# Three due times of an attention and expert schedule: 17 to 17.2, 33.7 to 33.2 and 65.7 to 65.2 heads

## The chip, the core and the metric

One core of one Trainium2 chip runs the kernel. TensorE (PE in the profile) multiplies; its weight loads have a row of their own (PEld). VectorE (DVE), ScalarE (ACT) and GpSimd (POOL) do the elementwise work, and SyncE (SP) issues nearly all of the DMAs. The metric is the device time of one execution in microseconds (us), the median of several runs. A profile is taken of one further execution; its span runs from the first to the last instruction.

## The reference

```python
scores = scale * np.matmul(q, k.transpose(0, 1, 3, 2))    # q, k, v: 8 batches, 8 heads, 576 x 64
mask = block_i >= block_j                                 # blocks of 64 positions
scores = np.where(mask, scores, -1000000000.0)
scores = scores - np.max(scores, axis=-1, keepdims=True)
attn = np.exp(scores)
attn = attn / (np.sum(attn, axis=-1, keepdims=True) + 1e-09)
x = np.matmul(attn, v)                                    # then laid out as 4608 tokens x 512
h = x @ w_in                                              # 512 x 2048
g = h * (1.0 / (1.0 + np.exp(-1.702 * h)))
out = g @ w_out                                           # 2048 x 512
```

Block-causal attention on 64 heads feeds a two-layer feed-forward part, all in float32. A token's row of `x` needs all 8 heads of its batch.

## The kernel before

**Attention.** The 64 heads are taken two at a time, in 32 turns (`step(n)`). A turn scores five query chunks of pair n, named 0 to 4: chunk i has up to 128 queries and 64·(2i+1) keys. `score` multiplies into PSUM banks; `weigh` adds the mask and finds the row's extreme on DVE (L351) and takes the exponential on ACT (L358); `normalise` makes the reciprocal of the sum on DVE (L368, L371) and scales on POOL (L376) or, in late turns, for chunk 4 on DVE (L378). In late turns `turn` transposes the weights on DVE (L385, L390), and sixteen DMAs behind chunk 4 finish the transposition. `av(n-1)` (item V) multiplies the previous pair's weights with its values, and ACT copies the result into a ring of tokens `xr` (L450, L451). `prep(n+1)` (item L) transposes the next pair's q and k on DVE (L297) into one buffer `qk`.

**Order within a turn.** A string says at which slot each item stands. Pairs 0 to 3 and 4 to 7 have their own (with PE transposes a, B, C instead of DVE's), pair 8 has `HANDOVER`, and pairs 9 to 31, the late turns, have

```python
    "3+0/2+1 - - - V - - 4 - - - L -",
```

that is 13 slots: chunks 3, 0, 2, 1 at slot 0, V at slot 4, chunk 4 at slot 7, L at slot 11.

**Experts.** The tokens are cut into 12 tiles of 384, each tile into 16 chunks (`fc`) of 128 columns of `w_in`. To keep float32's accuracy each operand is split into a high and a low part, so a product takes three matmuls. A chunk of experts is 12 matmuls into one bank `hp` (tag "h", a single buffer), then ACT's tanh (L562), DVE's product `g` (L563), ACT's `gh` (L571), POOL's `gl` (L82), and later 9 matmuls into three banks `acc` (`second`, which runs behind the next chunk's `hp`). The next chunk's first `hp` matmul writes the bank that L563 reads, so it waits for L563. When a tile changes, `split` casts new tokens to `xh` on ACT (L498) and takes the remainder `xl` on DVE (L82); `xh` and `xl` are single buffers too. A tile may be split only when all heads of its batches are done (`heads_for`).

**What mixes the two.** `moe()` is a generator that emits chunks. Behind every slot of a turn `advance` draws from it until the planned time `state["t"]` has reached a limit `quota(pos)`; `pos` counts heads (2 to a turn). In late turns it stops only at a gate, which stands behind the 12 `hp` matmuls of a chunk, so attention items enter PE's order only there. `quota` interpolates between pairs of heads and tiles:

```python
TILES_BY = ((8.4, 0), (17, 1), (33.7, 4), (65.7, -2))
        return -1.0 if pos < xs[0] else np.interp(pos, xs, [ends[y if y >= 0 else y - 1] for y in ys])
```

A tile's planned time is 16 equal chunks; -2 stands for the end of the tenth tile. The 11th and 12th tiles need all 64 heads and come last, with no attention beside them. PE's matmuls keep the order in which they are emitted (`keep_in_program_order`). On DVE, ACT and POOL the framework orders the instructions by priority (L562, L563, L571 and `split` have a higher one), and each engine then runs its own in that order.

Of the kernel before, what the change touches and what calls it, by code (L numbers as in the profile page):

```python
# [33 lines left out]


WEIGHTS_BY = ((0, 0), (8, 13), (14.5, 32))
TILES_BY = ((8.4, 0), (17, 1), (33.7, 4), (65.7, -2))


@with_exitstack  # L40
def attention_moe_kernel(
# [540 lines left out]
    def quota(pos):  # L582
        xs, ys = zip(*TILES_BY)
        return -1.0 if pos < xs[0] else np.interp(pos, xs, [ends[y if y >= 0 else y - 1] for y in ys])
# [80 lines left out]
```

## Time and profile before

| | |
|---|---|
| time, median of 3 runs | 1123.53 us (1121.69 to 1123.55) |
| the profiled execution's own time | 1120.49 us |
| its span | 1118.6 us |
| PE, PEld busy | 1076.4 us (96%), 908.7 us (81%) |
| DVE, ACT, POOL busy | 583.0 us (52%), 498.6 us (45%), 406.7 us (36%) |
| mean granted TensorE clock | 0.992 |

Matmuls overlap in the records, so the time that a group of matmuls takes on PE is best read from the start of its first to the start of the next group. A row of a timeline gives the start, the time of the group, the engine and line, the operation, the tile written and those read, their shapes, and in brackets the idle time just before, with what ended it. A row of windows gives for each stretch its length, then each engine's busy time with the number of instructions, the granted TensorE clock, the DMA engines' mean share and GB/s.

### The profile page before, as it was taken

To read this page: it belongs to the slowest core of one execution; us is meant where nothing else is said; L and a number is where in the kernel's file an instruction comes from. 1 tells how busy PE (TensorE), PEld (TensorE's weight loads), DVE (VectorE), ACT (ScalarE), POOL (GpSimd) and SP (SyncE) were. 2 spreads that over 40 slices of the span, in tenths; PEclk is the share of its full clock that TensorE was granted. 3 is DMA by queue.
4 is the path that set the end of the run, shared out by engine and by line. 5 is a ranking of instruction groups with operands and counts; after the bars stand their busy time and mean duration, and the time that the engine had idled before them with its cause. 6 is when DMAs were issued, how large, how long until landed. Compare 5 with 4: busy or idle time off the path is not lost. (4 is left out here: it accounts for less than half of the span.)

```text
span 1118.6 us, 19977 instructions
## 1 busy us (share of the span) xinstructions
PE 1076.4 (96%) x6960; PEld 908.7 (81%) x6960; DVE 583.0 (52%) x1856; ACT 498.6 (45%) x1321; POOL 406.7 (36%) x509
## 2 busy tenths in 40 slices
PE   5969998999999999999999999999999999999998
PEld 3757776788888888888888888888888888899997
DVE  6776885545545555654555655645545654211210
ACT  5866776434534433534443543444434444322322
POOL 4665664333333332333333333333333233122222
PEclk9979999999999999999999999999999999999999
DMA  8734532332444432343443333344342332200000
GB/s 171 205 89 153 150 73 62 84 79 57 105 86 86 103 80 64 64 98 78 98 101 74 75 93 65 70 108 85 81 107 63 71 85 58 54 29 1 29 1 29
DMA packets 219365, 91.25 MB, mean 82 GB/s; under 512 B 197760, under 2 KB 197760, under 8 KB 219264
## 3 DMA queue, kind: packets, MB, share of 16 engines
q1 hardware_dynamic: 214528, 89.38, 34.0%
q10 hardware_dynamic: 4736, 0.59, 0.3%
q8 instruction: 55, 0.90, 0.3%
q14 instruction: 46, 0.38, 0.1%
HBM read 45.09 MB, written 9.44 MB: 49 GB/s over the span
## 5 line engine op out<-in xcount | busy, mean ns | idle before, releaser
L82 POOL TENSOR_TENSOR gl<-g,gh 128x384 fp32r<-128x384 f32 x192 | 194.7, 1014 | 551.5 <-ACT gh L571 449.1
L99 PE MATMUL hp<-xh,wih 128*128 128x384 f32 x768 | 264.7, 345 | 7.9 <-DVE g L563 6.9
L563 DVE SCALAR_TENSOR_TENSOR g<-g,hp 128x384 f32<-128x384 f32 x192 | 105.9, 552 | 319.1 <-ACT g L562 317.8
L99 PE MATMUL hp<-xh,wil 128*128 128x384 f32 x768 | 258.4, 336 | 0.1
L562 ACT ACTIVATE g<-hp 128x384 f32<-128x384 f32 x192 | 94.1, 490 | 359.8 <-PE hp L99 354.8
L99 PE MATMUL hp<-xl,wih 128*128 128x384 f32 x768 | 253.9, 338 | 0.4 <-DVE xl L82 0.4
L99 PE MATMUL acc<-woh,gh 128*128 128x512 f32 x576 | 233.9, 406 | 0.0
L99 PE MATMUL acc<-wol,gh 128*128 128x512 f32 x576 | 226.9, 394 | 0.0
L99 PEld LDWEIGHTS hp<-xh,wih 128*128 128x128 f32 x768 | 144.2, 188 | 34.1 <-DVE g L563 23.1
L99 PE MATMUL acc<-woh,gl 128*128 128x512 f32 x576 | 167.9, 393 | 0.3 <-POOL gl L82 0.3
L571 ACT CAST gh<-g 128x384 fp32r<-128x384 f32 x192 | 98.4, 513 | 156.5 <-DVE g L563 156.4
L99 PEld LDWEIGHTS hp<-xh,wil 128*128 128x128 f32 x768 | 144.3, 188 | 6.5 <-POOL wil L82 0.7
L358 ACT ACTIVATE e<-e,mx 64x64 f32<-64x64 f32 (+4 forms) x240 | 132.3, 552 | 37.6 <-DVE mx L351 37.6
L376 POOL TENSOR_TENSOR e<-e,sm 64x64 f32<-64x64 f32 (+1 forms) x192 | 113.6, 612 | 95.0 <-DVE sm L371 46.5
L99 PEld LDWEIGHTS hp<-xl,wih 128*128 128x128 f32 x768 | 143.6, 188 | 1.3 <-DVE xl L82 1.3
L99 PE MATMUL bank<-qk 64*128 64x320 f32 (+4 forms) x768 | 122.5, 428 | 14.5 <-DVE qk L297 11.1
L99 PEld LDWEIGHTS acc<-woh,gh 128*128 128x128 f32 x576 | 107.9, 187 | 34.2 <-issue 10.5
L99 PEld LDWEIGHTS acc<-woh,gl 128*128 128x128 f32 x576 | 107.8, 188 | 25.9 <-POOL gl L82 1.2
L99 PEld LDWEIGHTS acc<-wol,gh 128*128 128x128 f32 x576 | 108.3, 188 | 16.7 <-POOL wol L82 0.3
L351 DVE CUSTOM_DVE_ANT_0 e<-bank,mask 64x64 f32<-64x64 f32 (+4 forms) x240 | 89.7, 417 | 56.9 <-PE bank L99 52.8
L385 DVE STREAM_TRANSPOSE turned<-e 128x384 f32<-128x384 f32 (+1 forms) x192 | 92.3, 499 | 48.8 <-POOL e L376 48.3
L99 PEld LDWEIGHTS bank<-qk 64*128 64x128 f32 x768 | 69.6, 193 | 54.2 <-issue 25.4
(50 smaller groups left out, 956.0 us busy)
## 6 DMA issues: line engine op xcount, KB each, us to landing
turned<-turned SPq DMA_DIRECT2D x192, 80.0 KB, 2.1
turned<-turned SPq DMA_DIRECT2D x96, 112.0 KB, 2.2
raw<-in_q_dram SPq DMA_DIRECT2D x128, 72.0 KB, 2.4
out_dram<-osb SPq DMA_DIRECT2D x36, 256.0 KB, 2.2
raw<-in_k_dram SPq DMA_DIRECT2D x120, 72.0 KB, 2.6
turned<-turned SPq DMA_DIRECT2D x96, 88.0 KB, 2.1
words<-in_moe_w_in_dram SPq DMA_DIRECT2D x16, 512.0 KB, 6.3
vp<-in_v_dram SPq DMA_DIRECT2D x60, 128.0 KB, 2.4
```

What stands on the lines that cost most here:

```text
L82: eng.tensor_tensor(out=out, in0=in0, in1=in1, op=ALU.subtract)
L99: return tc.keep_in_program_order(nc.tensor.matmul(**kw))
L351: nc.vector.tensor_tensor_reduce(out=e[0:m, hd, lo:hi], in0=s, in1=mk, op0=ALU.add, op1=ALU.min, scale=-0.125, scalar=3e38 if lo == 0 else ...
L358: nc.scalar.activation(out=e[0:m, hd], in_=e[0:m, hd], func=AF.Exp, scale=-1.0, bias=mx[0:m, i, hd : hd + 1], accum_out=sm[0:m, i, hd : hd ...
L376: nc.gpsimd.tensor_tensor(out=x, in0=x, in1=sc.to_broadcast([m, width(i)]), op=ALU.mult)
L385: nc.vector.transpose(out=tw[:, :, SLOT[i] : SLOT[i] + i, hd].rearrange("p b j c -> p j b c"), in_=e[:, hd, 0 : i * P],)
L562: nc.scalar.activation(out=g, in_=hp[:, 0:tt], func=AF.Tanh, scale=1.702)
L563: nc.vector.scalar_tensor_tensor(out=g, in0=g, scalar=1.0, in1=hp[:, 0:tt], op0=ALU.add, op1=ALU.mult)
L571: nc.scalar.copy(out=gh, in_=g)
```

## The change

```diff
-TILES_BY = ((8.4, 0), (17, 1), (33.7, 4), (65.7, -2))
+TILES_BY = ((8.4, 0), (17.2, 1), (33.2, 4), (65.2, -2))
```

Tile 0 is spread over 8.8 heads instead of 8.6. Tiles 1 to 3 get 16 heads instead of 16.7, which is 48/16 = 3 chunks a head or six a turn, where it was 48/16.7 = 2.87 or 5.75 a turn. Tiles 4 to 9 keep 32 heads, six chunks a turn, but start half a head earlier. The work itself is the same: as many matmuls, elementwise instructions and DMAs of the same shapes.

In the late turns DVE's order shows it. These are the rows around the start of chunk 4 in the turn of pair 22 (`turned<-e` is the end of chunks 2 and 1, `e,mx<-bank,mask 128x256` the first scores of chunk 4, `g<-g,hp` a chunk of experts). Before:

```order
L385 STREAM_TRANSPOSE turned<-e 128x2x4x32 x2
L390 STREAM_TRANSPOSE turned<-e 64x2x2x32
L563 SCALAR_TENSOR_TENSOR g<-g,hp 128x384
L351 ISA e,mx<-bank,mask 128x256
L351 ISA mx 128x1
L563 SCALAR_TENSOR_TENSOR g<-g,hp 128x384
```

With the change:

```order
L385 STREAM_TRANSPOSE turned<-e 128x2x4x32 x2
L390 STREAM_TRANSPOSE turned<-e 64x2x2x32
L351 ISA e,mx<-bank,mask 128x256
L351 ISA mx 128x1
L563 SCALAR_TENSOR_TENSOR g<-g,hp 128x384
```

One chunk's L563 no longer stands between the end of chunks 2 and 1 and chunk 4: chunk 4 comes one chunk of experts earlier.

Behind chunk 4 in the same turn, before:

```order
L297 STREAM_TRANSPOSE qk<-raw 128x576 x2
L368 TENSOR_SCALAR sm<-sm 128x2
L371 RECIPROCAL sm<-sm 128x2
L378 TENSOR_SCALAR e<-e,sm 128x576 x2
L385 STREAM_TRANSPOSE turned<-e 128x4x4x32 x2
L390 STREAM_TRANSPOSE turned<-e 64x2x2x32
L563 SCALAR_TENSOR_TENSOR g<-g,hp 128x384 x2
```

With the change:

```order
L297 STREAM_TRANSPOSE qk<-raw 128x576
L368 TENSOR_SCALAR sm<-sm 128x2
L371 RECIPROCAL sm<-sm 128x2
L378 TENSOR_SCALAR e<-e,sm 128x576 x2
L385 STREAM_TRANSPOSE turned<-e 128x4x4x32 x2
L390 STREAM_TRANSPOSE turned<-e 64x2x2x32
L563 SCALAR_TENSOR_TENSOR g<-g,hp 128x384
L297 STREAM_TRANSPOSE qk<-raw 128x576
L563 SCALAR_TENSOR_TENSOR g<-g,hp 128x384 x2
```

The second half of L moved behind the first L563, and three L563 instead of two follow before the next turn's scores.

The third place is the start of tile 7, in the turn of pair 24, again on DVE. With the change the rows of chunk 3's end and of the new tile are

```order
L563 SCALAR_TENSOR_TENSOR g<-g,hp 128x384
L82 TENSOR_TENSOR xl<-xr,xh 128x384 x3
L385 STREAM_TRANSPOSE turned<-e 128x3x4x32
L563 SCALAR_TENSOR_TENSOR g<-g,hp 128x384
L385 STREAM_TRANSPOSE turned<-e 128x3x4x32
L351 ISA e,mx<-bank,mask 128x192
```

and, some rows further,

```order
L385 STREAM_TRANSPOSE turned<-e 128x2x4x32
L82 TENSOR_TENSOR xl<-xr,xh 128x384
L385 STREAM_TRANSPOSE turned<-e 128x2x4x32
```

where before all four `xl` stood together behind chunks 2 and 1 (`L82 TENSOR_TENSOR xl<-xr,xh 128x384 x4`). The tile now starts on either side of V: three quarters of its tokens' columns are split ahead of V's result and the last quarter behind it. Also, one of chunk 3's two transposes stands ahead of the second L563 here; before, both stood behind it.

## The prediction

> **What bounds the kernel now.** First the profile's page, its span, its busy times and the slices.
>
> ```profile
> span 1118.6 us, 19977 instructions
> PE 1076.4 (96%) x6960; PEld 908.7 (81%) x6960; DVE 583.0 (52%) x1856; ACT 498.6 (45%) x1321; POOL 406.7 (36%) x509
> PE   5969998999999999999999999999999999999998
> ```
>
> PE is busy nearly throughout, and the work on it is the same after the change. So the time can move only by what PE stands still or waits inside its queue. The second view is the waits, cut to PE. From 218 to 445 us (pairs 9 to 15) it has this one row:
>
> ```profile
> PE hp L99 <- DVE g L563: 5.1, 6, 0.9
> ```
>
> Six waits of 0.85 us each; from 445 to 930 us (pairs 16 to 31) the same view has none. The third view is windows, cut at the first score matmul of a turn: two turns, three turns and fourteen turns, each turn of six chunks of experts.
>
> ```profile
> core 0: us, PE busy (x) PEld busy (x) DVE busy (x) ACT busy (x) POOL busy (x), PEclk, DMA share, GB/s
> 252.37:318.17 65.80, 64.09 (x421) 54.74 (x420) 35.76 (x118) 28.00 (x75) 21.64 (x28) 1.00 0.37 84
> 346.20:444.83 98.63, 96.09 (x631) 82.05 (x630) 52.88 (x175) 40.26 (x109) 32.42 (x42) 1.00 0.38 86
> 472.78:923.98 451.20, 450.89 (x2942) 381.94 (x2941) 247.47 (x818) 189.45 (x511) 151.36 (x196) 1.00 0.38 85
> ```
>
> A turn is 65.80/2 = 32.90 us and 98.63/3 = 32.88 us in the first two, and 451.20/14 = 32.23 us in the last, for the same matmuls at a granted clock of 1.00. So a turn with the wait costs 0.66 us more than one without (the rest of the 0.85 us comes back as small queueing that the others have). The question is which kind of turn the change makes.
>
> **What makes the wait.** A turn that has it, from chunk 4's matmuls on (PE, then ACT, then DVE):
>
> ```profile
> 429.81 1.24 PE L99 MATMUL bank<-qk 64*128 64x256 f32 x8
> 438.36 0.44 PE L99 MATMUL hp<-xh,wih 128*128 128x384 f32 x1 [0.85 <-DVE g L563]
> 435.52 0.49 ACT L562 ACTIVATE g<-hp 128x384 f32<-128x384 f32 x1 [0.73 <-PE hp L99]
> 430.90 0.31 DVE L390 STREAM_TRANSPOSE turned<-e 64x128 f32<-64x128 f32 x1
> 431.35 0.43 DVE L351 CUSTOM_DVE_ANT_0 e<-bank,mask 128x256 f32<-128x256 f32 x1
> 433.45 0.77 DVE L297 STREAM_TRANSPOSE qk<-raw 128x576 f32<-128x576 f32 x1
> 435.22 0.95 DVE L378 TENSOR_SCALAR e<-e,sm 128x576 f32<-128x576 f32 x2
> 437.42 0.31 DVE L390 STREAM_TRANSPOSE turned<-e 64x128 f32<-64x128 f32 x1
> 437.75 0.55 DVE L563 SCALAR_TENSOR_TENSOR g<-g,hp 128x384 f32<-128x384 f32 x1
> ```
>
> DVE ends the transposes of chunks 2 and 1 only at 431.2, so chunk 4's first score instruction starts at 431.35. The tanh of the next chunk of experts is done at 436.0, but its L563 stands in DVE's order behind all of chunk 4 and starts at 437.75. The bank `hp` is read out at 438.3, and PE's next `hp` matmul starts at 438.36. A turn without the wait:
>
> ```profile
> 752.74 1.24 PE L99 MATMUL bank<-qk 64*128 64x256 f32 x8
> 760.44 0.45 PE L99 MATMUL hp<-xh,wih 128*128 128x384 f32 x1
> 749.82 0.55 DVE L563 SCALAR_TENSOR_TENSOR g<-g,hp 128x384 f32<-128x384 f32 x1
> 753.47 0.42 DVE L351 CUSTOM_DVE_ANT_0 e<-bank,mask 128x256 f32<-128x256 f32 x1 [3.10 <-PE bank L99]
> 759.83 0.56 DVE L563 SCALAR_TENSOR_TENSOR g<-g,hp 128x384 f32<-128x384 f32 x1
> ```
>
> Here DVE had stood idle for 3.10 us and took chunk 4 up 0.73 us after its first matmul (1.54 us above). L563 starts 7.09 us after that matmul, against 7.94 us above: the difference is the 0.85 us of the wait. There is no slack to spare: the `hp` matmul follows at 7.70 us, just when L563 is through.
>
> **The change: where chunk 4 lands.** The limit in chunks is 64 + 3(pos − 33.7) = 3·pos − 37.1 in late turns before, and 16 + 3(pos − 17.2) = 3·pos − 35.6 with the change. An item goes in at the first gate that is not below the limit, so only the fraction counts: 0.1 below a whole number before, 0.6 below with the change. Six chunks over 13 slots put V at 6·4/13 = 1.85 chunks into the turn, chunk 4 at 6·7/13 = 3.23 and L at 6·11/13 = 5.08. Less 0.1 and rounded up they go in behind 2, 4 and 5 chunks; less 0.6, behind 2, 3 and 5. So chunk 4 moves from two chunks behind V to one. That is the first order shown above: one L563 fewer between the transposes and chunk 4. The waiting turns above have this spacing (the one shown, of pair 15, shares its DVE order behind chunk 4 with the second order shown above); at 5.75 chunks a turn the fraction drifts, and pairs 9, 10, 11, 13, 14 and 15 fell on it. With the change all 23 late turns do. In none of the turns of before with that spacing was the wait missing.
>
> **The sum.** Six waiting turns become at most 23: 17 × 0.66 = 11.2 us. Two corrections. First, the wait depends on DVE's order around chunk 3:
>
> ```profile
> 419.03 0.56 DVE L563 SCALAR_TENSOR_TENSOR g<-g,hp 128x384 f32<-128x384 f32 x1 [0.40 <-ACT g L562]
> 423.21 0.55 DVE L563 SCALAR_TENSOR_TENSOR g<-g,hp 128x384 f32<-128x384 f32 x1 [3.63 <-ACT g L562]
> 423.69 1.03 DVE L385 STREAM_TRANSPOSE turned<-e 128x384 f32<-128x384 f32 x2
> 424.86 0.36 DVE L351 CUSTOM_DVE_ANT_0 e<-bank,mask 128x192 f32<-128x192 f32 x1
> ```
>
> DVE idles 3.63 us, then has both transposes of chunk 3 (1.03 us) before chunks 2 and 1. In eight of the new turns (pairs 10, 13, 16, 19, 21, 24, 27, 29) one of the two stands ahead of that L563, in the idle time, as in the third order shown above. That brings what follows 0.5 us forward, so I take the excess down from 0.66 to 0.2 us there (bounds: 0 if all of it is absorbed, 0.66 if nothing). 15 × 0.66 + 8 × 0.2 = 11.5 us, less the six of before, 4.0 us: 7.5 us.
>
> Second, tiles 4 and 7 now start around V, as tile 1 does before:
>
> ```profile
> 204.37 0.45 PE L99 MATMUL hp<-xl,wih 128*128 128x384 f32 x1 [0.40 <-DVE xl L82]
> 204.66 0.39 PE L99 MATMUL acc<-woh,gh 128*128 128x512 f32 x1
> 203.63 0.69 DVE L82 TENSOR_TENSOR xl<-xr,xh 128x384 fp32r<-128x384 f32 x1
> ```
>
> The last quarter of `xl` waits for V's copy and for DVE's transposes, and PE for it: 0.40 us there. In a late turn V's matmuls are followed sooner, and I put the price at 0.4 to 1.2 us each, taking 0.7; 2 × 0.7 = 1.4 us. Tile 10 starts around the last V, with no scores on DVE in its way: 0. Tiles 3, 6 and 9 start behind chunk 4 (pairs 13, 21, 29): four `xl` stand ahead of L563 there and chunk 4's transposes behind it, so the one takes the other's place; bounds 0 and 0.7 us each, I add 0.2, together 0.6 us. Sum of the late turns: 7.5 + 1.4 + 0.6 = 9.5 us.
>
> The front changes as well: tile 0's 16 chunks are laid over 8.8 heads. The idle time that it could win or lose is in these windows:
>
> ```profile
> 84.00:112.00 28.00, 26.58 (x146) 21.02 (x144) 17.75 (x53) 17.85 (x47) 15.43 (x17) 1.00 0.49 153
> 112.00:140.00 28.00, 26.23 (x189) 21.30 (x189) 22.45 (x59) 20.08 (x53) 18.83 (x21) 1.00 0.58 151
> 140.00:168.00 28.00, 27.38 (x192) 21.47 (x191) 22.79 (x60) 20.59 (x54) 19.30 (x21) 1.00 0.31 72
> 168.00:191.00 23.00, 19.59 (x151) 15.79 (x149) 12.27 (x38) 14.22 (x37) 11.08 (x10) 1.00 0.31 75
> 191.00:219.00 28.00, 25.58 (x171) 20.54 (x170) 17.18 (x59) 12.77 (x35) 8.87 (x12) 1.00 0.23 63
> ```
>
> 1.42 + 1.77 + 0.62 + 3.41 + 2.42 = 9.6 us. About a third of a chunk (16·7.6/8.6 = 14.1 against 16·7.6/8.8 = 13.8 by head 16) moves behind the handover, and the items fall between other matmuls. I take 0, with 3 us either way, a third of the idle time. The end is unmoved: tiles 11 and 12 run alone in both.
>
> The profiled execution would go from 1120.49 to 1130.0 us. The median of the runs shown is 3.0 us above that execution, so for a median 1123.53 + 9.5 = **1133 us**.
>
> **A check by another measure.** The weight loads are busy 54.74 + 82.05 = 136.79 us of 164.43 in the five waiting turns, 83.2%, and 381.94 of 451.20, 84.65%, in the others; at the higher share the five would take 161.6 us, 0.57 us less each. The Trainium skill (Perfetto Trace Analysis, Identifying the Most-Contended Engine) holds matmul busy time for a bad measure, since matmuls are pipelined, and wants the share of weight loads instead. The trace bears that out: by PE's idle time a turn would lose 0.85 us, which gives 17 × 0.85 = 14.5 us before corrections, by weight loads 17 × 0.57 = 9.7 us.
>
> **The rivals.**
> *Every turn waits in full* (0.15): the moved transpose of chunk 3 does not help, since POOL's scaling and ACT's exponentials still end when they did, and the tile starts cost 1.2 us: 11.2 + 2.4 + up to 2 of the front, about 15 us, 1139 us. For it: chunks 2 and 1 wait on POOL in every turn. Against: these waits follow their own scores, which start earlier.
> *The front pays for it* (0.09): with flip and scores apart at the handover, 6 to 8 of the 9.6 us of idle time vanish, and the net is within 2 us: 1124 to 1126 us. Against: the items there wait for each other's banks and for POOL, not for experts.
> *Equal turns settle* (0.06), the other side: the place is DVE ahead of chunk 4. If in steady state chunks 2 and 1 are through before chunk 4's first bank, that is 0.85 us earlier than at 431.2, every late turn takes 32.23 us and the six waits go: −4.0 us, 1119.5 us. Three such turns in a row (346 to 445 us) each kept the wait, 32.88 us on average, which speaks against it.
>
> **How the numbers follow.** The forecast has 0.70, at 5 to 13 us more. What this kernel's measurement can tell from no change is about 0.2%, 2.2 us. Slower by more: forecast, full waits and a part of the front's case, 0.87; within: 0.08; faster: 0.05. The range leaves out the settled turns and the front's case below, and reaches to full waits above: 1126 to 1139 us.
>
> **What would show it.** In the profile after: PE's waits on L563 some 15 to 23 times instead of 6 between 218 and 930 us, 0.3 to 0.9 us each; L563 behind chunk 4 starting 7.5 to 8 us after chunk 4's first matmul; turns of 32.4 to 32.9 us from start to end of the late turns; the clock still 1.00. It is wrong if late turns take 32.2 us, if the waits are in the view but the turn's length is not longer, or if the stretch up to the first late turn (218.95 us) ends more than 3 us off.

## The result, and the profile after

The changed kernel takes 1129.63 us (median of 6 runs, 1128.72 to 1131.65) against 1123.94 us before (median of 6, 1121.69 to 1124.98): a ratio of 1.0061, with a 95% interval of 1.0050 to 1.0072, that is 5.6 to 8.1 us slower; the medians themselves lie 5.7 us apart. The prediction's 1133 us was 3.4 us too much, and its change of 9.5 us too large; sign, place and mechanism were as forecast.

PE's waits, from 218 to 950 us of the changed kernel (engine, line and what it waited for: us in all, times, the longest):

```profile
PE hp L99 <- DVE g L563: 15.9, 20, 1.2
PE hp L99 <- DVE xl L82: 1.6, 2, 0.8
```

Six waits on L563 have become twenty (one more, in pair 31, comes behind 950 us), and two waits on a new tile's `xl` are new. Windows of the changed kernel, cut like those of before: pair 10, pairs 14 and 15, pair 16 (where tile 4 starts), pair 21 (tile 6), and all of pairs 10 to 30:

```profile
252.31:284.73 32.42, 32.03 (x212) 27.35 (x211) 18.09 (x60) 13.92 (x38) 10.81 (x14) 1.00 0.35 74
383.96:449.75 65.79, 64.08 (x422) 54.73 (x421) 34.02 (x114) 24.59 (x68) 21.63 (x28) 1.00 0.39 90
449.75:482.90 33.15, 32.28 (x211) 27.37 (x210) 19.01 (x61) 15.79 (x41) 10.81 (x14) 1.00 0.33 70
614.03:646.65 32.62, 32.03 (x212) 27.36 (x211) 18.85 (x61) 15.29 (x41) 10.80 (x14) 1.00 0.30 64
252.31:942.53 690.22, 673.36 (x4412) 574.63 (x4411) 373.01 (x1229) 284.44 (x770) 227.12 (x294) 1.00 0.37 82
```

The ordinary late turn is 65.79/2 = 32.90 us, the waiting turn of before. Over pairs 10 to 30 a turn is 690.22/21 = 32.87 us, where before the later ones took 32.23. The clock is 1.00 in all. The rows of a turn (pair 14) are those of the old waiting turn: chunk 4's first matmul, DVE's end of chunks 2 and 1 and its first score instruction, ACT's tanh of the next chunk of experts, that chunk's L563, and the `hp` matmul that waits for it.

```profile
401.82 1.24 PE L99 MATMUL bank<-qk 64*128 64x256 f32 x8
402.91 0.31 DVE L390 STREAM_TRANSPOSE turned<-e 64x128 f32<-64x128 f32 x1
403.36 0.43 DVE L351 CUSTOM_DVE_ANT_0 e<-bank,mask 128x256 f32<-128x256 f32 x1
407.53 0.49 ACT L562 ACTIVATE g<-hp 128x384 f32<-128x384 f32 x1 [0.74 <-PE hp L99]
409.76 0.55 DVE L563 SCALAR_TENSOR_TENSOR g<-g,hp 128x384 f32<-128x384 f32 x1
410.37 0.44 PE L99 MATMUL hp<-xh,wih 128*128 128x384 f32 x1 [0.85 <-DVE g L563]
```

Chunk 4 is taken up 1.54 us after its first matmul, L563 starts 7.94 us after it though the tanh was done at 408.02, and PE waits 0.85 us: the same three figures as in the old waiting turn.

One thing is needed to read the totals. In the executions of these two kernels the mean granted clock varies from 0.986 to 0.992, and the span goes with it: the kernel before had spans of 1118.6 us at 0.992, 1120.1 to 1120.3 at 0.991, 1121.8 to 1122.1 at 0.988 and 1122.7 to 1123.6 at 0.986. (One execution of it, 1867.76 us at a clock of 0.748, enters no ratio.) The profiled execution of before was at 0.992 and that of after at 0.988, so their spans (1118.6 and 1129.4 us) differ by more than the kernels do. At equal clocks the change costs 8.3 to 8.5 us at 0.992 (1126.9 and 1127.1 us), 7.2 to 8.1 us at 0.991 (1127.5 and 1128.2 us) and 7.3 to 8.1 us at 0.988 (1129.4 and 1129.9 us).

### The profile page after: what moved, and what is told of

The parts are those of the page before. It is cut to its first block, busy times and chain, and to the rows that moved or that the text cites. A ratio compares the mean times of both kernels' runs of the same rounds, so it can differ in the third digit from the quotient of the medians.

```text
span 1129.4 us, 20020 instructions
## 1 busy us (share of the span) xinstructions
PE 1077.4 (95%) x6960; PEld 914.6 (81%) x6960; DVE 585.3 (52%) x1856; ACT 497.9 (44%) x1321; POOL 407.0 (36%) x509
## 5 line engine op out<-in xcount | busy, mean ns | idle before, releaser
L82 POOL TENSOR_TENSOR gl<-g,gh 128x384 fp32r<-128x384 f32 x192 | 194.6, 1014 | 560.7 <-ACT gh L571 442.7
L563 DVE SCALAR_TENSOR_TENSOR g<-g,hp 128x384 f32<-128x384 f32 x192 | 106.0, 552 | 337.0 <-ACT g L562 335.8
L99 PEld LDWEIGHTS acc<-wol,gh 128*128 128x128 f32 x576 | 108.3, 188 | 17.2 <-issue 0.9
L351 DVE CUSTOM_DVE_ANT_0 e<-bank,mask 64x64 f32<-64x64 f32 (+4 forms) x240 | 89.9, 417 | 12.9 <-PE bank L99 6.4
```

The costliest lines, as they stand in the source:

```text
L82: eng.tensor_tensor(out=out, in0=in0, in1=in1, op=ALU.subtract)
L99: return tc.keep_in_program_order(nc.tensor.matmul(**kw))
L351: nc.vector.tensor_tensor_reduce(out=e[0:m, hd, lo:hi], in0=s, in1=mk, op0=ALU.add, op1=ALU.min, scale=-0.125, scalar=3e38 if lo == 0 else ...
L563: nc.vector.scalar_tensor_tensor(out=g, in0=g, scalar=1.0, in1=hp[:, 0:tt], op0=ALU.add, op1=ALU.mult)
```

## The experiments

**Spacing without pacing.** The times of before; chunk 4 one slot earlier.

```diff
-    "3+0/2+1 - - - V - - 4 - - - L -",
+    "3+0/2+1 - - - V - 4 - - - - L -",
```

> The kernel before with its own pacing; only chunk 4 stands one slot earlier in the late turns (slot 6 instead of 7), which puts it one chunk of experts behind V in all of them. Theory (the spacing makes the wait): PE waits on L563 about 20 times instead of 6 between 218 and 930 us, late six-chunk turns of 32.9 us, in all 8 to 11 us more than before (ratio 1.007 to 1.010). Rival (the faster pacing itself costs, by more expert work in a turn or by the half head): within 0.2% of before.

Measured: 1133.83 us against 1123.63 us, ratio 1.0090 (1.0066 to 1.0114), about 10 us more. PE's waits in its late turns:

```profile
PE hp L99 <- DVE g L563: 18.0, 22, 1.1
```

And the window of two of them:

```profile
477.62:543.40 65.78, 64.06 (x422) 54.71 (x421) 34.03 (x114) 24.58 (x68) 21.65 (x28) 1.00 0.39 88
```

The old times make the new loss as soon as chunk 4 stands one chunk behind V. The spacing is enough.

**Pacing without spacing.** The new times; chunk 4 two slots later, two chunks behind V. (That is slot 9 in the count used above, from 0; the expectation's slot 10 counts from 1.)

```diff
-    "3+0/2+1 - - - V - - 4 - - - L -",
+    "3+0/2+1 - - - V - - - - 4 - L -",
```

> The changed kernel's pacing, with chunk 4 moved to slot 10 of the late turns, so that it comes two chunks behind V as in the later turns of before. Theory: the waits on L563 go, late turns of 32.2 us, 10 us less than the changed kernel and 3 to 5 us less than before (ratio 0.995 to 0.998). Rival (the pacing itself costs): within 2 us of the changed kernel, 1127 to 1131 us.

Measured: 1122.00 us, ratio to before 0.9984 (0.9975 to 0.9993), 0.8 to 2.8 us less. PE's waits in its late turns:

```profile
PE hp L99 <- DVE xl L82: 4.1, 2, 2.0
PE hp L99 <- DVE g L563: 0.3, 2, 0.2
```

Windows of four plain turns, and of the turns of pairs 16 and 24:

```profile
480.74:609.51 128.77, 128.76 (x842) 109.12 (x841) 69.84 (x232) 52.56 (x143) 43.24 (x56) 1.00 0.37 81
444.74:480.74 36.00, 33.86 (x211) 28.43 (x210) 19.19 (x61) 16.00 (x41) 10.80 (x14) 0.95 0.37 89
705.93:740.27 34.34, 32.31 (x211) 27.32 (x210) 19.11 (x61) 15.80 (x41) 10.82 (x14) 1.00 0.40 94
```

The waits on L563 are gone and plain turns take 128.77/4 = 32.19 us, so the pacing itself costs nothing there. The gain is about half of the 3 to 5 us expected, because the tile starts around V are dear in this order: their two turns are 3.8 and 2.1 us longer, with 4.1 us of waits on `xl` (a part of the 3.8 us lies in a clock of 0.95 there). That much of the rival holds: in this order the tile starts, which the new times put at V, cost several us.

**The cause doubled.** The new times, chunk 4 directly behind V.

```diff
-    "3+0/2+1 - - - V - - 4 - - - L -",
+    "3+0/2+1 - - - V 4 - - - - - L -",
```

> The changed kernel with chunk 4 directly behind V (slot 5), no chunk of experts between: the suspected cause doubled. Theory: DVE cannot end chunks 2 and 1 earlier, so chunk 4's first score instruction waits for it and L563 comes 3 to 4 us after the bank is wanted, in every late turn: turns of 35.5 to 36 us and 60 to 75 us more in all, about 1195 us. Rival (the wait has to do with the three chunks behind chunk 4 or with the tiles' starts): within 5 us of the changed kernel.

Measured: 1199.58 us, one execution, at a mean clock of 0.974. The window of two turns:

```profile
686.13:757.20 71.07, 66.77 (x421) 56.41 (x420) 34.03 (x114) 24.45 (x68) 21.61 (x28) 0.98 0.35 79
```

PE's waits over all its late turns:

```profile
PE hp L99 <- DVE g L563: 29.0, 18, 2.7
PE bank L99 <- ACT xr L451: 18.8, 22, 0.9
PE bank L99 <- DVE mx L351: 7.9, 17, 0.7
```

71.07/2 = 35.5 us a turn, at the edge of what was expected. The size was right and its parts were not: of the 55.7 us in these rows only 29.0 are waits on L563. The rest is score matmuls waiting for a bank, behind V's copy on ACT (L451) or behind DVE's reading of other scores (L351). So with no chunk between, the banks are late too.

**L563 ahead of chunk 4's end.** The new times and the new spacing as they are; chunk 4's sum, scaling and transposes are emitted one slot later and pinned behind what DVE was given last, the next chunk's L563.

```diff
-    "3+0/2+1 - - - V - - 4 - - - L -",
+    "3+0/2+1 - - - V - - 4 T - - L -",
...
+    def finish(n):
+        e = late.pop(n)
+        normalise(n, NCH - 1, e, True)
+        turn(n, NCH - 1, e)
...
+                if n > 2 * HP and i == NCH - 1:
+                    late[n] = e[i]
+                    continue
...
+        if pin:
+            tc.keep_in_program_order(d)
```

The new item T calls `finish`, and `d` is L368 of chunk 4.

> The changed kernel with pacing and spacing unchanged; chunk 4's sum, scaling and transposes are emitted one slot later and held behind the next chunk's L563 on DVE. Theory (L563 is late because it stands in DVE's order behind all of chunk 4): waits on L563 go, late turns of 32.2 us or a little less, 10 us less than the changed kernel, about 1118 to 1120 us. Rival (the bank or V's copies on ACT are what is late, whatever DVE's order): the waits stay and the time is that of the changed kernel.

Measured: 1109.57 us, ratio to before 0.9873 (0.9859 to 0.9888), 14 us less than before and 20 us less than the changed kernel. PE's waits in its late turns (its L575 is L563 of the others):

```profile
PE hp L99 <- DVE xl L82: 2.1, 2, 1.1
PE hp L99 <- DVE g L575: 0.6, 3, 0.2
```

The window of four plain turns:

```profile
474.66:601.78 127.12, 127.12 (x841) 109.80 (x840) 72.75 (x232) 52.56 (x143) 43.50 (x56) 1.00 0.38 82
```

The timeline of one of them from chunk 4's first matmul on (L359 is L351, L388 is L378):

```profile
492.52 1.24 PE L99 MATMUL bank<-qk 64*128 64x256 f32 x8
494.06 0.42 DVE L359 CUSTOM_DVE_ANT_0 e<-bank,mask 128x256 f32<-128x256 f32 x1
498.76 0.56 DVE L575 SCALAR_TENSOR_TENSOR g<-g,hp 128x384 f32<-128x384 f32 x1 [1.16 <-ACT g L574]
499.63 1.71 DVE L388 TENSOR_SCALAR e<-e,sm 128x576 f32<-128x576 f32 x2
```

Chunk 4 is taken up 1.54 us after its first matmul, as late as in the waiting turns, yet PE does not wait in this turn: now DVE waits 1.16 us for ACT ahead of L563, and chunk 4's scaling comes after it. So the wait came from L563's place in DVE's order. The rival, that the bank or V's copies are late, falls. The gain was expected at 10 us and is 20: a plain turn takes 127.12/4 = 31.78 us, 0.45 us less than the turns that show no wait of PE at all. L563 had held those too, in pieces that the view cut to PE does not show. Cut to PE's weight loads it does; this is its row in the fourteen turns of the kernel before, from 472.78 to 923.98 us:

```profile
PEld hp L99 <- DVE g L563: 11.1, 28, 0.6
```

That is two waits a turn of 0.40 us each, and the four turns of the held kernel have none. In pair 23 of the kernel before, one of the fourteen, L563 ends at 685.89 and 695.87 us, and the `hp` matmuls behind it start at 685.95 and 695.93. 23 × 0.45 us is the 10 us that were not expected.

**The first time alone.** 17 to 17.2, the others as before.

```diff
-TILES_BY = ((8.4, 0), (17, 1), (33.7, 4), (65.7, -2))
+TILES_BY = ((8.4, 0), (17.2, 1), (33.7, 4), (65.7, -2))
```

> The kernel before with the first of the three times alone changed, 17 to 17.2 (33.7 and 65.7 stay). By the trace of the change its front, up to the first scores of pair 8, is 2.5 us shorter than the front of before at the same granted clock, and five late turns have chunk 4 one chunk behind V instead of six. Theory: 3 us less than before (0.1 to 0.4% less), and 5 waits on L563. Rival (the front's gain is a difference between executions): within 1 us of before.

Measured: 1119.18 us against 1125.00 us, ratio 0.9950 (0.9933 to 0.9967). That is more than the 0.1 to 0.4% expected, but the two sets of executions differ in clock, six of the seven of before having 0.986. At 0.992 the spans are 1115.7 and 1118.6 us, 2.9 us less; at 0.989 they are 1117.2 and 1120.6 to 1122.1 us, 3.4 to 4.9 us less. There are 5 waits on L563. So the front's gain is real, by what was read off the trace or somewhat more.

**The late times alone.** 33.2 and 65.2, the first as before.

```diff
-TILES_BY = ((8.4, 0), (17, 1), (33.7, 4), (65.7, -2))
+TILES_BY = ((8.4, 0), (17, 1), (33.2, 4), (65.2, -2))
```

> The kernel before with the second and third of the times alone changed, 33.2 and 65.2 (17 stays). Chunk 4 then comes one chunk behind V in 20 late turns (pairs 12 to 31) instead of 6. Theory: 14 more turns at 0.66 us, less some 2 us where a transpose of chunk 3 stands ahead of L563: 6 to 9 us more than before, 18 to 20 waits on L563. Rival (the first time is what costs): within 2 us of before.

Measured: 1133.09 us against 1123.85 us, ratio 1.0090 (1.0068 to 1.0112), with 17 waits on L563 up to 950 us (18 up to 980) and 2 on `xl`. At a clock of 0.989 the spans of the same set are 1131.2 and 1131.4 us against 1121.9 and 1122.0, 9.2 to 9.5 us more, just above the 6 to 9 expected. So the change is a loss of some 9 us by the late times and a gain of some 3 us by the first. The two give 4 to 7 us, less than the 7.2 to 8.5 us of all three; they need not add up exactly, since the new spacing is in 20 late turns under the late times alone and in 23 under all three.

**Six chunks at the old fraction.** Six chunks in every late turn, chunk 4 two chunks behind V.

```diff
-TILES_BY = ((8.4, 0), (17, 1), (33.7, 4), (65.7, -2))
+TILES_BY = ((8.4, 0), (17.7, 1), (33.7, 4), (65.7, -2))
```

> Six chunks of experts in every late turn, as the change has it, but at the fraction of before: the times are 17.7, 33.7 and 65.7. Theory (not the six chunks but the half head lost the time): no wait on L563 above 0.3 us, late turns of 32.2 us, 4 us less than before, with the front unknown by 3 us either way: 1117 to 1123 us. Rival (six chunks in the turns of pairs 9 to 15 cost): above 1125 us.

Measured: 1116.82 us, ratio 0.9930 (0.9915 to 0.9946), just below the expected 1117; at a clock of 0.991 it is 5.6 to 6.3 us less than before (1114.0 and 1114.5 us). There is one wait of 0.2 us on L563. Its 22 late turns of pairs 9 to 30:

```profile
212.37:920.91 708.54, 708.29 (x4621) 599.98 (x4620) 389.21 (x1286) 298.36 (x804) 237.93 (x308) 1.00 0.38 85
```

708.54/22 = 32.21 us each. Six chunks in every late turn are good; the half head that came with them in the change was not.

**The same hold, under other times.** The hold of chunk 4 that gained 20 us was tried with the times of before and with the first alone at 17.2. There chunk 4 comes a chunk later in most turns, and its end had to be emitted a slot later still to stand behind a chunk of experts.

```diff
-    "3+0/2+1 - - - V - - 4 - - - L -",
+    "3+0/2+1 - - - V - - 4 - T - L -",
```

Both runs have this order and the `finish` and pin shown above; the second has 17.2 beside.

> The three times of before, with chunk 4's sum, scaling and transposes held behind the next chunk's L563 as in the run before it of that kind. Theory (all that the new times lose in late turns is L563's place): late turns of 31.8 us whether chunk 4 comes one or two chunks behind V, 12 to 15 us less than before, and so within 3 us of the same edit under the new times (1109.6 us). Rival (the spacing costs something beside): 4 us or more below it.

> The first time alone changed to 17.2, and chunk 4 held behind L563. Theory: the front's 2.5 us and the held chunk 4 add up, without the tile starts around V, which cost the run with the new times 2.7 us: 1106 to 1108 us. Rival (the front's gain is not real): 1109 to 1111 us.

Measured: 1158.72 us (ratio 1.0311, 1.0284 to 1.0338) and 1155.00 us (1.0279, 1.0257 to 1.0302). Both expectations and both rivals missed, by 44 us and more. PE's waits in the late turns of the first, but for one of 0.5 us on L563:

```profile
PE bank L99 <- DMA turned<-turned: 16.9, 10, 2.3
PE bank L99 <- DMA raw<-in_q_dram: 9.5, 4, 2.6
PE bank L99 <- issue: 7.9, 4, 2.4
```

The timeline from the end of one turn's chunk 4 to the next V, on DVE, SP's queue and PE:

```profile
543.88 0.31 DVE L400 STREAM_TRANSPOSE turned<-e 64x128 f32<-64x128 f32 x1
543.88 10.06 SPq L407 DMA_DIRECT2D turned<-turned  x16
555.70 0.52 PE L99 MATMUL bank<-turned,vp 128*64 128x128 f32 x7 [1.49 <-DMA turned<-turned]
```

PE hardly waits for L563 now, but for V's operands. All eighteen of these waits stand ahead of V's first matmul, whatever releaser the view names. SP issues the sixteen DMAs of the transposed weights one after the other in 10.06 us. They start at 543.88, the last goes out near 553.9, and V, for which PE was ready at 555.70 − 1.49 = 554.2, starts at 555.70. In the run at 1109.57 us the sixteen have one more chunk's time before V:

```profile
502.57 11.23 SPq L407 DMA_DIRECT2D turned<-turned  x16
517.02 1.22 PE L99 MATMUL bank<-turned,vp 128*64 128x128 f32 x22
```

Issued by 513.80, they are in place when V starts at 517.02, with no wait. The first run bears this out within itself: its pairs 10, 11, 14 and 15, where chunk 4 comes one chunk behind V, as it does in the turn ahead of each, take 31.78 us each, and its later turns of six chunks, with chunk 4 two behind V, 33.3 to 36.1 us. That the sixteen DMAs are what V waits for is read off the trace; no run changed them alone. So the hold needs the earlier chunk 4 that the change brings, and the change needs the hold.

**The hold, with tile starts off V.** The times 17.867, 33.867 and 65.867 with the hold at its first slot: the new spacing, tiles 4 and 7 two chunks later. Against the kernel of 1109.57 us:

```diff
-TILES_BY = ((8.4, 0), (17.2, 1), (33.2, 4), (65.2, -2))
+TILES_BY = ((8.4, 0), (17.867, 1), (33.867, 4), (65.867, -2))
```

> Chunk 4's sum, scaling and transposes held behind the next L563, six chunks in every late turn at the fraction of the change, but all three times 0.667 head later (17.867, 33.867, 65.867), so that tiles 4 and 7 start two chunks later, off V. Theory: turns of 31.8 us without exception; the five turns that were 0.5 to 1.35 us longer at tile starts lose that, 4 us in all, the front is up to 2 us longer: 1104 to 1109 us. Rival (the tile starts cost the same wherever they stand, or V waits for the transposed weights): 1110 us or more.

Measured: 1112.23 us, ratio to before 0.9908 (0.9887 to 0.9929). That misses the expected 1104 to 1109 us and lies where the rival's number is, but not for the rival's reasons: the turns at tile starts are 0.3 to 0.5 us longer than 31.78 instead of 0.5 to 1.35, which is worth some 2 us (4 were expected), and in all late turns V waits for the transposed weights once, 0.3 us. The loss is in the handover turn, that of pair 8. Its window, and in it the second half of chunk 4's scores:

```profile
185.91:213.05 27.14, 23.21 (x149) 18.07 (x148) 17.91 (x60) 12.80 (x35) 8.18 (x12) 0.87 0.15 32
203.58 1.43 PE L99 MATMUL bank<-qk 64*128 64x320 f32 x2 [3.43 <-DVE mx L359]
```

It takes 27.14 us and has 148 weight loads, where the run at 1109.57 us has 168 in 27.73 us and no wait above 1.33 us. So PE waits 3.43 us there for a bank that DVE reads. The granted clock is 0.87 in this window and 1.00 in the other, so a part of the loss is the clock's, and how much was not separated. By the medians the best kernel of the study stays the one with the new times and the hold, 1109.57 us.

## Why the prediction was right

**Where chunk 4 lands.** Right. It predicted 15 to 23 waits instead of 6 and turns of 32.4 to 32.9 us; there are 20 in the view and the turns of pairs 10 to 30 take 32.4 to 33.3 us. The longest wait is 1.2 us, where 0.9 was the most expected. That this spacing makes the loss is shown from both sides, by the runs with spacing alone and pacing alone.

**The price of a waiting turn, 0.66 us.** Right: plain turns take 32.90 us against 32.23.

**The eight turns with a transpose ahead, 0.2 us.** Right where nothing else happens: pair 10's 32.42 us is 0.19 us over 32.23, and pairs 19 and 27 take the same.

**Tile starts.** Pairs 16 and 24 were put at 0.2 + 0.7 = 0.9 us and are 33.15 − 32.23 = 0.92 us over, nearly all of it in the `xl` waits of 0.8 us each, as at tile 1 before but twice as long; these two turns have no wait on L563. Pairs 13, 21 and 29 were put at 0.4 us and are 0.57, 0.39 and 0.40 us over.

**Missed in the late turns.** Pairs 11, 12 and 28 take 33.16 to 33.27 us, 0.3 us more than a plain waiting turn. In pair 11 DVE stands idle for 0.50 us ahead of chunk 4's first score instruction, behind a wait that the view puts to DVE itself, and starts it 1.89 us after chunk 4's first matmul instead of 1.54. In pairs 12 and 28 DVE waits 1.00 us for POOL's scaling of chunk 1, where it is 0.71 in other turns. In all three PE then waits 1.14 to 1.21 us on L563 instead of 0.85. Why DVE and POOL start later there stays open; it is 0.9 us in all.

**The front, 0 with 3 us either way.** This is the term that was mis-sized: the first time gains some 2.5 to 3 us. At the same mean clock of 0.93, the first scores of pair 8 start at 189.55 us with the change and at 193.59 us in the run with the spacing alone, which has the old times: 4.0 us earlier, of which the eight matmuls that now come later (the third of a chunk that the prediction saw move) are some 1.4 us. The rest of the span, from the first scores of pair 9 to the end, in a window of before and one of the changed kernel:

```profile
218.95:1118.60 899.65, 890.26 (x5626) 763.50 (x5625) 427.86 (x1384) 354.92 (x927) 284.19 (x357) 1.00 0.31 71
```

```profile
217.29:1129.40 912.11, 889.76 (x5635) 766.44 (x5634) 429.15 (x1384) 353.74 (x927) 285.11 (x358) 1.00 0.31 71
```

That is 12.5 us more, of which nine `hp` matmuls of 0.175 us, 1.6 us, had been done ahead of that point before: 10.9 us, against 9.5 us summed. Less 2.5 us of the front it is 8.4 us, as found at equal clocks.

So the late turns were summed 1.4 us too low and the front 2.5 us too high, and that these partly cancel is luck: 8.4 us against 9.5. The remaining distance to the 5.7 us between the medians is in no term of the sum. The median of before, 1123.94 us, is what that kernel takes at a clock of 0.988 (1123.67 to 1123.99 us in its executions there), and that of the changed kernel, 1129.63 us, what it takes at 0.991 (1129.31 and 1129.96 us). The rival in which the front pays for all of it asked for 6 to 8 us.

**The measure by weight loads.** It gave 0.57 us a turn, near the 0.66 us. What it showed beside was not followed up: the turns without a wait stood at 84.65%, and the kernel with L563 first reaches 109.80/127.12 = 86.4% in its plain turns, while matmul busy time called both full (450.89 of 451.20 us, and 127.12 of 127.12). The Trainium skill (Perfetto Trace Analysis, Identifying the Most-Contended Engine) calls matmul busy time a bad measure, because matmuls are pipelined. The traces here agree that it is one: 0.45 us a turn was hidden in it.

**"There is no slack to spare."** The prediction saw that L563 was just in time in the turn without a wait, and took 32.23 us for a turn that loses nothing. The held kernel's 31.78 us, and the weight loads' two waits a turn, show that it was late there as well. The sum was not hurt, since both kinds of turn share it.

## What to carry to other kernels

When a planner's numbers shift work by a fraction, work out where each item lands after rounding up, and look in the old trace for turns that already stood so: they give the price without a model. A short instruction that frees the only buffer of the busiest engine should not stand in an in-order queue behind a long chain; putting it ahead of that chain was worth more (20 us) than all the pacing. And before holding a chain back, look at what hangs on its end: here sixteen DMAs, some 10 us of issuing, which fit only because the same change had brought the chain forward.

## What the runs showed of the hardware that was not expected

SP needs 0.63 to 0.70 us for each of the sixteen small DMAs in the turns shown (10.06/16 and 11.23/16), so that the issuing, more than the landing (2.1 us, the median), sets when the last one is in place. The granted clock at the start differs between executions of the same program. The run with the spacing alone has the program of before up to pair 8. These are the first 28 us of before and of that run:

```profile
0.00:28.00 28.00, 16.18 (x82) 10.45 (x84) 18.77 (x72) 16.57 (x50) 13.59 (x29) 0.94 0.87 171
0.00:28.00 28.00, 16.18 (x84) 11.05 (x86) 18.84 (x72) 16.52 (x50) 13.65 (x29) 0.88 0.88 174
```

The clock is 0.94 in one and 0.88 in the other, and up to the first scores of pair 8 the mean is 0.96 and 0.93. These come at 191.02 and 193.59 us, 2.6 us apart, as much as a whole term of the sum and a reason to compare spans at the same clock.
